# Sections in a norm, attention batches without a mutual wait, a slack in a planner and more idle matmuls: one kernel, four changes at once

## The chip, the cores and the metric

The kernel runs on one core of a Trainium2 chip. The metric is the device time of one execution in microseconds (us), lower is better. A "fast run" is an execution that shows no slow state; all runs below are fast but one of h1_normg. Ratios to the kernel before, with their 95% intervals in brackets, are taken from runs of the same rounds and are not quite the ratio of the medians that are quoted. In lines of the profile, PE is TensorE and PEld its loading of weights, ACT is ScalarE, DVE VectorE, POOL GpSimd and SP SyncE; SPq is the DMA queue of SP. The granted clock is the share of full clock that TensorE was given.

## The reference

Eight batches of linear attention with an RMS norm, and behind it a channel mixing of two branches:

```python
kv  = einsum('bhsd,bhse->bhde', k, v)              # 8 batches, 8 heads, 576 rows, 64 wide
o   = einsum('bhsd,bhde->bhse', q, kv)
x   = o / sqrt(mean(o*o, -1) + 1e-6) * g_norm      # per head; then heads side by side: 512 wide
xk  = mu_k*x + (1-mu_k)*x_prev                     # x_prev: the row before in the same batch
xr  = mu_r*x + (1-mu_r)*x_prev
out = sigmoid(xr @ w_r) * (max(xk @ w_k, 0)**2 @ w_v)   # 512 -> 1024 -> 512
```

In the kernel, "K", "V" and "R" are the matmuls with w_k, w_v and w_r, done for nine groups of 512 rows; "kv", "u", "st" (sums of squares), "rr" (the norm factor spread over a head's partitions) and "x" are the steps of attention, done for each of eight batches. A group needs one or two finished batches.

## The kernel before

The kernel is written as pieces of work. A planner in Python simulates them while the kernel is built, with a cost for each piece, a model of DMA, and a number of buffers for each name; its only product is which engine takes a piece and the order of the instructions on each engine. The order is then fixed: each engine takes its instructions one after the other, and one that has to wait holds up all behind it.

```python
class Planner:
    LAT = {"PE": 0.25, "ACT": 0.15, "DVE": 0.12, "POOL": 0.15, "SP": 0.0}
    SWITCH = {"PE": 0.11, "ACT": 1.28}
    SHUN = {"DVE": 0.5}
    STAY = {"PE": 4.0, "ACT": 4.0}
    # ... run():
                for eng, us in p.on.items():
                    t = max(free.get(eng, 0.0), room)          # engine free, buffers free
                    for d in p.deps:
                        t = max(t, d.end + (self.LAT[d.eng] if d.eng != eng or d.land else 0.0))
    # ... the earliest start wins; among those within 0.02 us of it, the smallest "due"
            if p.land:                                          # a DMA: when does it land?
                came = p.end + 1.2
                if p.eng == "POOL":                             # loads, one after the other
                    dma = max(dma, came) + p.land
                    p.end = dma + 0.8
                else:                                           # stores and transposing DMAs, on SP
                    p.end = max(came + p.land, min(dma, came + 2 * p.land)) + 0.8
                    dma = max(dma, came) + p.land
```

Until the first R matmul, gaps of TensorE in the plan are filled with matmuls of zeros ("idle matmuls"), which keep its clock up. The attention of a batch waits, besides its loads, for the last rr of the batch before (`last_rr[b - 1]`). Batches 0 to 2 have q transposed on TensorE, batches 3 to 7 by a DMA. The norm of a whole batch, four head pairs by 576 rows, works on one tile of 128 x 576, of which eight rows hold something:

```python
        mm = add({"PE": 0.25 * n}, kv_mm, mode=1, bufs=[pkv, kin, vin, kv], due=due(26),
                 deps=[loaded[...] ...] + [last_rr[b - 1]])
        # ...
        if b >= 3:
            m = add({"SP": 3.2}, q_dma, bufs=[qin, qT], due=due(30), deps=[loaded[("q", b, 0)]], land=2.5)
        # ... st_act:
            nc.scalar.activation(out=get(ln)[:, 0:wide, 0:w], in_=pst.t[:, 0:wide, 0:w], func=AF.Ln, bias=eps, scale=1.0 / HD)
            nc.scalar.activation(out=get(rs)[:, 0:wide, 0:w], in_=ln.t[:, 0:wide, 0:w], func=AF.Exp, scale=-0.5)
        st = add({"ACT": 0.42 + 0.0018 * sec}, st_act, deps=[m], bufs=[pst, ln, rs], due=due(17), mode="ln")
```

Of the kernel before, what the change touches and what calls it, by code (L numbers as in the profile page):

```python
# [25 lines left out]
class Piece:  # L26
    def __init__(self, on, fn, deps, bufs, due, land, mode):
        self.on, self.fn, self.due, self.land, self.mode = on, fn, due, land, mode
        self.deps = [d for d in deps if d is not None]
        self.bufs = list(bufs)  # L30
        for b in self.bufs:
            b.users.append(self)
        self.eng = self.start = self.end = None


class Planner:
# [3 lines left out]
    SHUN = {"DVE": 0.5}  # L40
    STAY = {"PE": 4.0, "ACT": 4.0}
# [5 lines left out]
    def add(self, on, fn, deps=(), bufs=(), due=0.0, land=0.0, mode=None):  # L47
        p = Piece(on, fn, deps, bufs, due, land, mode)
        self.left.append(p)
        return p  # L50
# [24 lines left out]
    def run(self, warm=None):  # L75

        free, order, dma, modes = {}, [], 0.0, {"PE": None, "ACT": None}
        while self.left:
            best = {}
            for p in self.left:  # L80
                if any(d.end is None for d in p.deps):
                    continue
                room = self.room(p.bufs)
                if room is None:
                    continue
                ways = []
                for eng, us in p.on.items():
                    t = max(free.get(eng, 0.0), room)
                    for d in p.deps:
                        t = max(t, d.end + (self.LAT[d.eng] if d.eng != eng or d.land else 0.0))  # L90
                    ways.append((t + us + self.SHUN.get(eng, 0.0), t, eng))
                _, t, eng = min(ways)
                stay = self.STAY.get(eng, 0.0) if p.mode == modes.get(eng) else 0.0
                best.setdefault(eng, []).append((t, p.due - stay, p))
# [5 lines left out]
            if warm and p.eng == "PE":  # L100
                since, until, idle = warm
                n = int((t - max(free.get("PE", 0.0), since)) / 0.23)
                if n > 0:
                    order.append(lambda n=n: idle(n))
                if p is until:
                    warm = None
# [29 lines left out]
def kernel(  # L136
# [22 lines left out]
    HS = S // 2  # L159
    NI = NJ // 2  # L160
# [18 lines left out]
        "ln": (1, (128, 2, HS), FP32),  # L179
        "rs": (2, (128, 2, HS), BF16),  # L180
# [41 lines left out]
    g_st = const.tile([128, 128], FP32, name="g_st")  # L222
    eps = const.tile([128, 1], FP32, name="eps")
    zeros = const.tile([128, 512], BF16, name="zeros")
    sel2 = const.tile([128, 32], BF16, name="sel2")
    selg = const.tile([128, NHP, 128], BF16, name="selg")
# [7 lines left out]
    def consts_small(_):  # L234
        nc.vector.memset(zeros, 0.0)
        nc.vector.memset(g_st, 0.0)
        nc.sync.dma_start(out=mu_raw[0:NHP], in_=moe_mu_k.rearrange("(j p) -> j p", p=128))
        nc.sync.dma_start(out=mu_raw[NHP:2 * NHP], in_=moe_mu_r.rearrange("(j p) -> j p", p=128))
        g_row = g_norm.rearrange("(o d) -> o d", o=1)
        for hp in range(NHP):  # L240
            for e in range(2):
                nc.sync.dma_start(out=g_st[32 * hp + e:32 * hp + e + 1, HD * e:HD * e + HD], in_=g_row)
        nc.vector.memset(eps, 1e-6)
        nc.vector.memset(selg, 0.0)

        nc.vector.memset(sel2, 0.0)
        for e in range(2):
            nc.vector.memset(sel2[64 * e:64 * e + 64, e:e + 1], 1.0)
        ln_table()
# [6 lines left out]
    def consts_mu(_):  # L256
# [5 lines left out]
        for hp in range(NHP):  # L262
            rows = slice(32 * hp, 32 * hp + 32)
            nc.vector.tensor_copy(out=selg[rows, hp, :], in_=g_st[rows])
# [4 lines left out]
    add({"DVE": 0.9}, consts_small, due=-1000)  # L269
# [6 lines left out]
    def load(b, n, h0, h1, due):  # L276
# [6 lines left out]
        p = add({"POOL": 0.8}, fn, bufs=[kvq[(n, b)]], due=due, land=(h1 - h0) * 0.36)  # L283
# [5 lines left out]
    for hp0, n in PARTS0:  # L289
        for name in ("k", "v", "q"):  # L290
            load(0, name, 2 * hp0, 2 * hp0 + 2 * n, -900 + hp0)
        if p_ident is None:
            p_ident = add({"POOL": 0.8}, consts_idents, due=-900 + 0.5)
    p_mu = add({"DVE": 0.5}, consts_mu, deps=[p_ident], bufs=[p_mu_ps], due=-800)
    p_wr = add({"POOL": 0.8}, lambda _: load_w(w_r_sb, moe_w_r), due=-700, land=2.6)
    p_wk = add({"POOL": 0.8}, lambda _: load_w(w_k_sb, moe_w_k), due=-699, land=5.2)
    for n in ("k", "v", "q"):
        load(1, n, 0, H, -698)
    p_wv = add({"POOL": 0.8}, lambda _: load_w(w_v_sb, moe_w_v), due=-697, land=5.2)
# [6 lines left out]
    last_rr = {-1: None, 0: None}  # L306
# [14 lines left out]
    def attention_part(b, part, bufs, ps_buf):  # L321
# [26 lines left out]
        def kv_copy(eng, e):  # L348
            for half in range(2):
# [3 lines left out]
        mm = add({"PE": 0.25 * n}, kv_mm, mode=1, bufs=[pkv, kin, vin, kv], due=due(26),  # L353
                 deps=[loaded[(m, b, h)] for m in ("k", "v") for h in (2 * hp0, 2 * (hp0 + n) - 1)] + [last_rr[b - 1]])
        kvs = [add({"DVE": 0.25 + 0.14 * n, "ACT": 0.38 + 0.11 * n}, lambda eng, e=e: kv_copy(eng, e), deps=[mm],
# [4 lines left out]
        if b >= 3:  # L360
# [4 lines left out]
            m = add({"SP": 3.2}, q_dma, bufs=[qin, qT], due=due(30), deps=[loaded[("q", b, 0)]], land=2.5)  # L365
            qts = {hp: m for hp in hps}
        else:
            for hp in hps:
# [7 lines left out]
                def q_cp(eng, hp, ps):  # L376
# [3 lines left out]
                m = add({"PE": 0.35}, lambda _, hp=hp, ps=ps: q_tr(_, hp, ps), bufs=[ps, qin, qT], due=due(27),  # L380
                        deps=[p_ident, loaded[("q", b, 2 * hp)], loaded[("q", b, 2 * hp + 1)], last_rr[b - 1]])
                qts[hp] = add({"ACT": 0.65, "DVE": 0.75}, lambda eng, hp=hp, ps=ps: q_cp(eng, hp, ps), deps=[m],
# [4 lines left out]
        for hp in hps:  # L387
# [17 lines left out]
            m = add({"PE": 0.14}, lambda _, hp=hp, ps=ps: u_mm(_, hp, ps), mode=1, deps=kvs + [qts[hp]],  # L405
                    bufs=[ps, kv, qT, uT, sq], due=due(22))
            us[hp] = add({"ACT": 0.69, "DVE": 0.75}, lambda eng, hp=hp, ps=ps: u_cp(eng, hp, ps), deps=[m],
                         bufs=[ps, uT], due=due(21))
            sqs.append(add({"DVE": 0.46}, lambda eng, hp=hp: u_sq(eng, hp), deps=[us[hp]], bufs=[uT, sq],
                           due=due(20)))  # L410



        nsec = NHP // n
        sec = S // nsec
        pst = ps_buf()
        wide = 2 if sec > 512 else 1
        w = sec // wide

        def st_mm(_):  # L420
            for x in range(wide):
                for i, hp in enumerate(hps):
                    for c in range(nsec):
                        row = 32 * (i * nsec + c)
                        nc.tensor.matmul(get(pst)[row:row + 32, x, 0:w], sel2,  # L425
                                         sq.t[:, hp, sec * c + w * x:sec * c + w * x + w], start=True, stop=True)

        def st_act(_):
            ln_table()
            nc.scalar.activation(out=get(ln)[:, 0:wide, 0:w], in_=pst.t[:, 0:wide, 0:w], func=AF.Ln, bias=eps,  # L430
                                 scale=1.0 / HD)
            nc.scalar.activation(out=get(rs)[:, 0:wide, 0:w], in_=ln.t[:, 0:wide, 0:w], func=AF.Exp, scale=-0.5)

        m = add({"PE": 0.3}, st_mm, mode=2, deps=sqs, bufs=[pst, sq, ln, rs], due=due(18))
        st = add({"ACT": 0.42 + 0.0018 * sec}, st_act, deps=[m], bufs=[pst, ln, rs], due=due(17), mode="ln")


        xms = []
        step = min(2, n)
        for hp1 in range(hp0, hp0 + n, step):  # L440
            for half in range(2):
# [3 lines left out]
                def rr_mm(_, hp1, half, ps):  # L445
                    for i in range(step):
                        c0 = HS * half
                        while c0 < HS * half + HS:
                            c, off = divmod(c0, sec)
                            x, off = divmod(off, w)  # L450
                            cnt = min(HS * half + HS - c0, w - off)
                            nc.tensor.matmul(get(ps)[:, i, c0 - HS * half:c0 - HS * half + cnt],  # L452
                                             selg[:, (hp1 - hp0 + i) * nsec + c, :], rs.t[:, x, off:off + cnt],
                                             start=True, stop=True)
                            c0 += cnt

                def x_mul(_, hp1, cs, xs, ps):
                    if xT.t is None:
# [7 lines left out]
                m = add({"PE": 0.13 * step}, lambda _, hp1=hp1, half=half, ps=ps: rr_mm(_, hp1, half, ps),  # L466
                        deps=[st, p_mu], bufs=[ps, rs, xT], due=due(14))
                xms.append(add({"DVE": 0.15 + 0.3 * step},
# [11 lines left out]
        df = add({"DVE": 0.4 * n}, diff, deps=xms, bufs=[xT, d], due=due(11))  # L480
# [3 lines left out]
        for pos, (key, dst, m) in enumerate(order):  # L484
# [15 lines left out]
            sc = add({"DVE": 0.365 * n, "ACT": 0.7 * n}, lambda eng, m=m, t=t: scale(eng, m, t), deps=[df, p_mu], bufs=[d, t], due=late)  # L500
            x_ready[b][key].append(add({"DVE": 0.06 + 0.34 * n}, lambda _, dst=dst, t=t: blend(_, dst, t), deps=[sc],
# [18 lines left out]
    p_first = add({"PE": 0.01}, lambda _: None, deps=x_ready[0]["r"] + [p_wr], bufs=[warm], due=-1)  # L520
    hold = add({"PE": 0.01}, lambda _: None, bufs=[warm], due=-2000)

    def mix(g):
# [23 lines left out]
        for f2 in range(NFC // 2):  # L547
            ps, rt, u = Buf("mm"), Buf("relu"), k0 + 2 * f2
            ms = []
            for x in range(2):  # L550
                ms.append(add({"PE": 0.865}, lambda _, fc=2 * f2 + x, ps=ps: k_mm(_, fc, ps),
                              deps=ms or need["k"] + [p_wk], bufs=[ps, sqk], due=u + x))
            a = add({"ACT": 1.04}, lambda _, ps=ps, rt=rt: k_relu(_, ps, rt), deps=ms[1:], bufs=[ps, rt], due=u + 2)
            sqs.append(add({"DVE": 0.7}, lambda _, f2=f2, rt=rt: k_sq(_, f2, rt), deps=[a], bufs=[rt, sqk], due=u + 4))
# [13 lines left out]
        for c2 in range(2):  # L568
            ps, sg, u = Buf("mm"), Buf("sig"), r0 + 2 * c2
            ms = []  # L570
            for x in range(2):
                ms.append(add({"PE": 0.865}, lambda _, ci=2 * c2 + x, ps=ps: r_mm(_, ci, ps),
                              deps=ms or need["r"] + [p_first], bufs=[ps, sg], due=u + x))
            sigs.append((sg, add({"ACT": 1.04}, lambda _, ps=ps, sg=sg: r_sig(_, ps, sg), deps=ms[1:], bufs=[ps, sg],
# [11 lines left out]
        for c2 in range(2):  # L586
# [3 lines left out]
            for x in range(2):  # L590
                for part in range(2):
                    ms.append(add({"PE": 0.865},
                                  lambda _, ci=2 * c2 + x, part=part, ps=ps: v_mm(_, ci, part, ps),
                                  deps=ms[-1:] or sqs + [p_wv, sg_done.deps[0]], bufs=[ps, sqk, ot], due=u + 2 * x + part))
            for xs in ((0, 2),) if g < NG - 1 else ((0, 1), (1, 2)):
                dv = add({"DVE": 0.12 + 0.56 * (xs[1] - xs[0])},
# [45 lines left out]
```

## Time and profile before

| | before |
|---|---|
| time | 239.06 us (median of 3 runs, 238.25 to 239.2) |
| span of the profiled run | 236.1 us |
| TensorE busy | 214.8 us, 91% |
| first R matmul | 28.2 us |
| end of the last V matmul | 231.7 us |

From the page of the kernel before, TensorE's busy time, its busy tenths in 40 slices of 5.9 us, the granted clock in tenths, and what DMA moved in each slice:

```profile
PE 214.8 (91%) x1538; PEld 100.4 (43%) x1538; DVE 137.3 (58%) x233; ACT 136.1 (58%) x184; POOL 25.2 (11%) x39
...
PE   2988999579987999989998998999899999999971
...
PEclk9999999857997999999999999999999999999997
...
GB/s 80 187 209 206 204 207 204 203 182 189 199 194 222 193 163 175 224 149 160 270 82 3 90 89 0 3 120 60 0 12 162 9 41 137 0 37 143 0 89 89
```

TensorE is busy almost throughout, and the clock line says where this is not full rate: slices 8, 9, 10 and 13, counted from one (41 to 59 us and 71 to 77 us). DMA moves about 200 GB/s until 100 us (163 to 224 in slices 2 to 17), and another line of the page has its engines busy 90% or more in these slices, all but the 15th.

The timeline of TensorE before, between 40 and 59 us (start, duration, line, operation, result <- operands, count, and in brackets the idle time before and what ended it):

```profile
40.34 1.90 PE L537 MATMUL mm<-xk,w_k 128*128 128x512 bf16 x8
43.93 0.65 PE L452 MATMUL at<-rs,selg 128*128 128x288 bf16 x4 [1.69 <-ACT rs L432]
45.18 0.40 PE L452 MATMUL at<-rs,selg 128*128 128x288 bf16 x2 [0.60 <-DVE xT L461]
...
49.26 1.49 PE L343 MATMUL at<-v,k 96*64 96x64 bf16 x48
...
52.30 1.08 PE L393 MATMUL at<-qT,kv 64*64 64x288 bf16 x7 [0.59 <-ACT kv L205]
53.31 1.89 PE L537 MATMUL mm<-xk,w_k 128*128 128x512 bf16 x4
...
58.62 1.03 PE L580 MATMUL mm<-w_v,sqk 128*128 128x512 bf16 x4
```

K of group 0 ends at about 42 us, and then only attention of batches 1 and 2 is left, in small pieces between waits: first for the norm on ScalarE (1.69 us), then for xT on VectorE. K of group 1 starts at 53.31 and V of group 0 at 58.62. The granted clock falls with the gaps.

The same view in a later batch: rr is eight matmuls, and the last four wait, two by two, for a buffer that x on VectorE has to free.

```profile
102.58 0.40 PE L452 MATMUL at<-rs,selg 128*128 128x288 bf16 x2 [0.60 <-DVE xT L461]
103.25 0.41 PE L452 MATMUL at<-rs,selg 128*128 128x288 bf16 x2 [0.26 <-DVE xT L461]
```

And what became of the q of batch 3: the transposing DMA on SP's queue starts at 53.44, and the load that waits for its end starts at 65.92 on POOL; the k load of batch 5 comes at 70.15.

```profile
53.44 6.82 SPq L362 DMA_TRANSPOSE qT<-q  x1
```

```profile
65.92 0.77 POOL L278 DMA_DIRECT2D q<-in_q_dram  x1 [13.33 <-DMA qT<-q]
...
70.15 0.77 POOL L278 DMA_DIRECT2D k<-in_k_dram  x1
```

TensorE asks for this q at 69.78 us, 4 us after it has landed.

```profile
69.78 0.44 PE L393 MATMUL at<-qT,kv 64*64 64x288 bf16 x8
```

### The profile page before, as it was taken

What the parts mean: (1) busy time and instruction counts of PE and PEld (TensorE: products, weight loads), DVE (VectorE), ACT (ScalarE), POOL (GpSimd) and SP (SyncE); (2) the same over time, 40 slices, a digit from 0 to 9 for tenths busy, and PEclk for the clock granted to TensorE, in tenths of its full rate; (3) what the DMA queues carried; (4) which work ended last, traced back from release to release, by engine and by line L of the source; (5) the groups of instructions that cost most, each with busy time, mean ns of one, the idle gap of its engine ahead of it and who ended that gap; (6) DMA issues with size and microseconds to landing.
All of it is one profiled execution on the core that took longest, in us unless ns stands there. A gap on an engine that the chain in (4) does not pass through costs nothing.

```text
span 236.1 us, 3800 instructions
## 1 busy us (share of the span) xinstructions
PE 214.8 (91%) x1538; PEld 100.4 (43%) x1538; DVE 137.3 (58%) x233; ACT 136.1 (58%) x184; POOL 25.2 (11%) x39
## 2 busy tenths in 40 slices
PE   2988999579987999989998998999899999999971
PEld 1443453253442453444444484434344444444430
DVE  2127936597698498379729953985596224224221
ACT  2075788585366857786688668855953603604500
POOL 8833030040031021001000000000000000000000
PEclk9999999857997999999999999999999999999997
DMA  5999999999999979999930320042005014015033
GB/s 80 187 209 206 204 207 204 203 182 189 199 194 222 193 163 175 224 149 160 270 82 3 90 89 0 3 120 60 0 12 162 9 41 137 0 37 143 0 89 89
DMA packets 38497, 29.41 MB, mean 125 GB/s; under 512 B 13384, under 2 KB 33360, under 8 KB 38480
## 3 DMA queue, kind: packets, MB, share of 16 engines
q0 software_dynamic: 21008, 16.78, 47.2%
q1 hardware_dynamic: 17472, 12.40, 23.1%
q8 instruction: 12, 0.20, 0.4%
q14 instruction: 5, 0.04, 0.1%
HBM read 33.56 MB, written 9.44 MB: 182 GB/s over the span
## 4 chain that ended last, share of the span: by engine, by line
PE 79%; DVE 10%; ACT 6%; issue 2%; POOL 1%; DVEq 0%; POOLq 0%
PE mm L537 27%; PE mm L580 25%; PE mm L560 12%; DVE xT L461 5%; PE mm L609 5%; PE at L393 3%; PE at L452 2%; PE at L343 2%; DVE out L584 2%; ACT t L493 1%; DVE d L478 1%; PE at L425 1%; ACT ln L430 1%; PE at L373 1%; ACT kv L205 1%
## 5 line engine op out<-in xcount | busy, mean ns | idle before, releaser
L537 PE MATMUL mm<-xk,w_k 128*128 128x512 bf16 (+1 forms) x320 | 69.2, 367 | 0.1
L580 PE MATMUL mm<-w_v,sqk 128*128 128x512 bf16 x288 | 65.5, 379 | 2.0 <-DVE out L584 1.7
L541 ACT ACTIVATE relu<-mm 128x1024 bf16<-128x1024 f32 x36 | 36.9, 1024 | 39.8 <-PE mm L537 39.1
L537 PEld LDWEIGHTS <-w_k 128*128 128x128 bf16 x320 | 30.0, 99 | 31.4 <-issue 4.0
L580 PEld LDWEIGHTS <-sqk 128*128 128x128 bf16 x288 | 27.6, 97 | 34.7 <-issue 3.7
L544 DVE TENSOR_TENSOR sqk<-relu 128x1024 bf16<-128x1024 bf16 x36 | 24.9, 691 | 29.4 <-ACT relu L541 29.4
L584 DVE TENSOR_TENSOR out<-mm,sig 128x1024 f32<-128x1024 f32 (+1 forms) x20 | 22.3, 1116 | 25.0 <-PE mm L580 24.9
L560 PE MATMUL mm<-w_r,xr 128*128 128x512 bf16 x144 | 32.9, 380 | 0.0
L461 DVE TENSOR_TENSOR xT<-uT,at 128x576 bf16<-128x576 bf16 (+1 forms) x31 | 21.1, 731 | 17.0 <-PE at L452 16.9
L493 ACT ACTIVATE t<-d,mu_sb 128x576 bf16<-128x576 bf16 x34 | 23.7, 764 | 4.0 <-DVE d L478 2.4
L560 PEld LDWEIGHTS <-xr 128*128 128x128 bf16 x144 | 13.5, 98 | 16.7 <-issue 1.3
L565 ACT ACTIVATE sig<-mm 128x1024 bf16<-128x1024 f32 x18 | 17.9, 1024 | 4.3 <-PE mm L560 4.2
L205 ACT CAST uT<-at 128x576 bf16<-128x576 f32 x23 | 13.9, 641 | 10.0 <-PE at L393 10.0
L609 PE MATMUL mm<-zeros 128*128 128x512 bf16 x64 | 18.0, 410 | 0.0
L452 PE MATMUL at<-rs,selg 128*128 128x288 bf16 (+1 forms) x62 | 11.1, 285 | 6.1 <-DVE xT L461 4.3
L205 ACT CAST kv<-at 64x256 bf16<-64x256 f32 x24 | 8.8, 366 | 12.9 <-PE at L343 12.5
L402 DVE TENSOR_TENSOR sq<-uT 128x576 bf16<-128x576 bf16 x32 | 13.9, 455 | 3.2 <-ACT uT L205 2.8
L278 POOL DMA_DIRECT2D q<-in_q_dram x10 | 7.5, 751 | 48.5 <-DMA qT<-q 31.4
L452 PEld LDWEIGHTS <-selg 128*128 128x128 bf16 x68 | 6.5, 97 | 12.9 <-issue 10.3
L393 PE MATMUL at<-qT,kv 64*64 64x288 bf16 x116 | 9.1, 316 | 2.8 <-ACT uT L205 0.9
L496 DVE TENSOR_TENSOR xk<-t,xT 128x2304 bf16<-128x2304 bf16 (+2 forms) x10 | 11.2, 1116 | 0.5 <-ACT t L493 0.4
L478 DVE TENSOR_TENSOR d<-xT 128x2304 bf16<-128x2304 bf16 (+2 forms) x10 | 11.2, 1119 | 0.3
(52 smaller groups left out, 135.0 us busy)
## 6 DMA issues: line engine op xcount, KB each, us to landing
out_dram<-out SPq DMA_DIRECT2D x24, 192.0 KB
k<-in_k_dram POOLq DMA_DIRECT2D x7, 576.0 KB, 14.3
v<-in_v_dram POOLq DMA_DIRECT2D x7, 576.0 KB, 16.4
q<-in_q_dram POOLq DMA_DIRECT2D x7, 576.0 KB, 7.7
out_dram<-out SPq DMA_DIRECT2D x24, 128.0 KB
out_dram<-out SPq DMA_DIRECT2D x24, 64.0 KB
w_k<-in_moe_w_k_dram POOLq DMA_DIRECT2D x1, 1024.0 KB, 12.3
w_v<-in_moe_w_v_dram POOLq DMA_DIRECT2D x1, 1024.0 KB, 23.3
```

The lines of the kernel that those rows point to most:

```text
L205: nc.scalar.copy(out=dst, in_=src)
L452: nc.tensor.matmul(get(ps)[:, i, c0 - HS * half:c0 - HS * half + cnt], selg[:, (hp1 - hp0 + i) * nsec + c, :], rs.t[:, x, off:off + cnt], ...
L461: nc.vector.tensor_mul(out=xT.t[:, hs, xs], in0=get(uT)[:, hs].rearrange("q h i jj p -> q h (i jj p)")[:, :, cs], in1=ps.t[:, 0:step, 0:HS])
L493: nc.scalar.mul(out=dst, in_=d.t[:, hp, :], mul=by)
L537: nc.tensor.matmul(get(ps)[:, fc % 2, a0:a1], w_k_sb[:, cc, 128 * fc:128 * fc + 128], xk[:, cc, x0:x0 + a1 - a0], start=(cc == 0), stop=(c ...
L541: nc.scalar.activation(out=get(rt), in_=ps.t, func=AF.Relu)
L544: nc.vector.tensor_mul(out=get(sqk)[:, 2 * f2:2 * f2 + 2, :], in0=rt.t, in1=rt.t)
L560: nc.tensor.matmul(get(ps)[:, ci % 2, :], xr[:, cc, n0:n0 + 128], w_r_sb[:, cc, :], start=(cc == 0), stop=(cc == NHP - 1))
L565: nc.scalar.activation(out=get(sg), in_=ps.t, func=AF.Sigmoid)
L580: nc.tensor.matmul(get(ps)[:, ci % 2, :], sqk.t[:, fc, 128 * ci:128 * ci + 128], w_v_sb[:, fc, :], start=(fc == 0), stop=(fc == NFC - 1))
L584: nc.vector.tensor_mul(out=get(ot)[:, xs, :], in0=ps.t[:, xs, :], in1=sg.t[:, xs, :])
L609: nc.tensor.matmul(get(warm)[:, 0, :], zeros[:, 0:128], zeros, start=True, stop=True)
```

## The change

Four things in one: (1) the norm is cut into four sections of 144 columns, so that ln and exp work on 128 x 144 (with a second buffer for ln); (2) only batch 1 waits for the rr of the batch before, the others run free; (3) the planner reckons 0.3 us of slack on everything that TensorE waits for; (4) the idle matmuls go on after the first R matmul, until 80 us of planned time, in the buffer that the next piece will write. The intent is a shorter norm, more freedom for the planner, and an order that waits less on the chip. The diff, cut to its core (names for the pieces and constants left out):

```diff
+    SLACK = {"PE": 0.3}
...
-                    t = max(free.get(eng, 0.0), room)
+                    slack = self.SLACK.get(eng, 0.0)
+                    t = max(free.get(eng, 0.0), room + slack)
                     for d in p.deps:
-                        t = max(t, d.end + (self.LAT[d.eng] if d.eng != eng or d.land else 0.0))
+                        t = max(t, d.end + (self.LAT[d.eng] + slack if d.eng != eng or d.land else 0.0))
...
+                gap = t - max(free.get("PE", 0.0), since)
+                if first is not None:
+                    n, buf = int(gap / 0.23), None
+                else:
+                    n, buf = int((gap - 0.3) / 0.23), p.bufs[0] if p.fresh and not p.bufs[0].placed else None
+                    n = n if buf is not None and t < until else 0
...
-    last_rr = {-1: None, 0: None}
+    last_rr = {}
...
-        mm = add(... deps=[loaded[...] ...] + [last_rr[b - 1]])
+        mm = add(... deps=[loaded[...] ...] + ([last_rr[0]] if b == 1 else []))
...      # the q transposes likewise
-        m = add({"PE": 0.3}, st_mm, mode=2, deps=sqs, bufs=[pst, sq, ln, rs], due=due(18))
-        st = add({"ACT": 0.42 + 0.0018 * sec}, st_act, ...)
+            for s in range(NHP):
+                for i, hp in enumerate(hps):
+                    tl, sub = place(i, s)
+                    nc.tensor.matmul(get(pst)[32 * tl:32 * tl + 32, 0, 0:SEC], sel[:, sub],
+                                     sq.t[:, hp, SEC * s:SEC * s + SEC], start=(sub == 0), stop=(sub == n - 1))
+            nc.scalar.activation(out=get(ln), in_=pst.t[:, 0, 0:SEC], func=AF.Ln, bias=eps, scale=1.0 / HD)
+            nc.scalar.activation(out=get(rs), in_=ln.t, func=AF.Exp, scale=-0.5)
+        st = add(f"rs {b}", {"ACT": 0.7}, st_ln, ...)
...
-                nc.sync.dma_start(out=g_st[32 * hp + e:32 * hp + e + 1, HD * e:HD * e + HD], in_=g_row)   # 8 of them
+        nc.sync.dma_start(out=g_all, in_=g_norm.rearrange("(o d) -> o d", o=1).broadcast_to([128, HD]))
...
-    plan.run((1.5, p_first, idle))
+    plan.run((1.5, p_first, 80.0, idle))
```

## The prediction

> # Prediction
>
> **What bounds it now.** TensorE: 214.8 of 236.1 us busy (page, part 1), 79% of the chain that ended last. By the timeline, 32 back-to-back 512-column matmuls take 6.91 us, 0.216 each (the Trainium skill, "TensorE: Matmul & The Clock Gate", Back-to-back issue gap, gives N/2.4 + 2.5 ns; the trace agrees). Nine groups of K, R and V, 80 such matmuls each, make 155.5 us. A batch of attention costs TensorE 0.88 (kv) + 1.1 (u) + 0.36 (statistics) + 0.9 (rr) = 3.25 us, and 1.3 us of transposes in batches 1 and 2: 25.5 us for seven. So 181 us of work lie between the first R (28.2 us) and the last V (231.7): about 22 us are lost there. Where, by timeline and windows:
> - 42 to 53.3 us: batch 1's blend is not done, batch 2 waits for batch 1's last rr. 3.2 us of work in 11.3: 8 lost. Granted clock 0.50 from 46 to 54.
> - 53 to 60: 1 us. 69.8 to 76.5: u waits for copies, then K at clock 0.5: 4 us.
> - Batches 3 to 6: 22.36 us a period against 17.3 + 3.25: 1.8 each, 7.4 us. Most is rr, 2.3 us instead of 0.9, as its at buffers wait for DVE xT (0.60 + 0.26 us).
> - Two waits of 0.84 us for DVE out at the end.
>
> **What the change does.**
> 1. Sectioned norm: ln and exp shrink from 128x576 (740 + 682 ns) to 128x144 (380 + 322 ns, as batch 0 shows). 0.72 us less ACT per batch, seven times, in each norm chain. TensorE's columns stay (8x288 becomes 16x144, twice); perhaps +0.1 us a batch. The selg build (four broadcast multiplies, estimated 0.6 to 0.8 us each from 691 ns for 128x1024 bf16 and 1222 for 128x1024 f32) falls in DVE's idle 5 to 11 us: free.
> 2. Batches from 2 on don't wait for the previous rr. Batch 2's loads land only about 39 to 44 us, so its kv comes some 5 us sooner, not more; it fills part of the hole.
> 3. Slack for TensorE: the planner puts V or K between rr pieces and before u. Takes most of the steady loss.
> 4. Idle matmuls until 80 us of planned time keep the clock up (same page, Part 1: a few us of idle halve the clock; here 0.50 after the gap at 42 to 44). Some will overstay; at the start the slack lengthens planned gaps, so the first R may come up to 1 us later.
>
> **Sum**, all where TensorE is critical: hole at 42 to 60: -4; 69 to 77: -2.5; steady: -4.5; start: +0.5; tail: 0. About -10.5. **Predicted 228.5 us, range 222 to 235.** Faster by over 2% 0.87, within 2% 0.10, slower by over 2% 0.03.
>
> **What would show it.** ln and rs at 380 and 322 ns throughout; PE's wait for xT at rr from 4.3 us to under 1.5; period of batches 3 to 6 about 21.2 us; more than 64 zeros matmuls, some after 30 us; clock 0.9 or more from 30 to 80 us; first K of group 1 before 52 us; first R at 28 to 29.
>
> **What would make it wrong.** Batch 2's copies (earlier due times) crowd DVE and ACT ahead of batch 1's blend, so the hole only moves; idle matmuls run while real work is ready; group 0's last squares, queued behind attention on DVE (relu done 44.8, square at 55), still block V; DMA, full until about 100 us, bounds batches 2 to 4; more ACT table loads (now 12 of 1.28 us).

## The result

The kernel after takes 245.51 us (median of 4, 245.15 to 247.04) against 239.13 us in the same rounds: ratio 1.0282, 95% interval 1.0228 to 1.0337. It is slower by 2.8%, where a gain of 4.4% was foreseen.

The page of the kernel after, the same lines (slices of 6.1 us):

```profile
PE 213.6 (88%) x1688; PEld 104.9 (43%) x1688; DVE 142.3 (58%) x246; ACT 125.5 (52%) x175; POOL 25.1 (10%) x39
...
PE   3999899899009989989999899999989999999981
...
PEclk9999999999657999999999999999999999999997
...
GB/s 43 198 209 205 204 207 204 204 204 200 161 177 184 255 172 198 206 213 76 6 156 110 3 112 62 3 0 175 0 0 117 58 0 172 3 11 164 0 86 86
```

TensorE's busy time is 1.2 us less in a span 7.2 us longer. Slices 11 and 12, counted from one (60.8 to 73.0 us), have a 0: TensorE stands still. The timeline of TensorE around it:

```profile
56.60 0.95 PE L354 MATMUL at<-v,k 96*64 96x64 bf16 x48
...
59.96 0.43 PE L433 MATMUL at<-sq,sel 128*32 128x144 bf16 x16
73.56 0.46 PE L404 MATMUL at<-qT,kv 64*64 64x288 bf16 x4 [13.17 <-DMA qT<-q]
...
74.35 1.17 PE L456 MATMUL at<-rs,selg 128*128 128x144 bf16 x8
75.31 1.06 PE L540 MATMUL mm<-xk,w_k 128*128 128x512 bf16 x2
```

Four u matmuls of batch 3, queued right behind the statistics of batch 2, wait 13.17 us for the DMA that transposes q. Behind them in the queue stand all of K of group 1 (its first piece starts at 75.31; before, it started at 53.31) and the rr of batch 2, though xk of batch 1 had been ready since 57.26 us. The chain that ended last, the profile's walk back from the last instruction to what released each one, says the same in its own columns (start, duration, what):

```profile
54.81 18.61 DMA qT<-q
73.43 0.14 issue
73.56 0.46 PE at L404 x4
```

The queues of SP and POOL, as shown of before:

```profile
54.81 7.88 SPq L373 DMA_TRANSPOSE qT<-q  x1
```

```profile
47.17 0.77 POOL L288 DMA_DIRECT2D k<-in_k_dram  x1 [2.31 <-PE at L354]
47.93 0.77 POOL L288 DMA_DIRECT2D v<-in_v_dram  x1
57.86 0.77 POOL L288 DMA_DIRECT2D k<-in_k_dram  x1 [9.15 <-PE at L354]
58.62 0.77 POOL L288 DMA_DIRECT2D v<-in_v_dram  x1
73.98 0.77 POOL L288 DMA_DIRECT2D q<-in_q_dram  x1 [14.60 <-DMA qT<-q]
```

The transposing DMA starts at 54.81, 1.4 us later than before, and lands at 73.43, 18.6 us after its start. Before, the load released by it came at 65.92, 12.5 us after its start. The difference is in what the queue of loads holds. In both kernels loads of batch 4 were still on their way when the transposing DMA was issued (1.6 MB of them before and 1.4 MB after, from a count of the bytes moved until then), but in the kernel after k and v of batch 5 came on top at 57.86 (1.18 MB), since the free-running kv of batch 3 had released their buffers early.

The kept trace has every DMA packet with its queue, size and time, which the views above do not split. The transposing DMA is 2304 packets of 256 B, and the first of them starts 4.0 us after the issue in both kernels. As long as loads are queued beside it, its packets and theirs (768 B) go one for one: 611 and 606 from 58.5 to 62 us before, 1383 and 1311 from 63 to 71 us after. Before, the loads ran out at 63.8 us, the rest of the transposing DMA then went at about 1000 packets a us instead of some 175, and its last packet was done at 64.7 us. After, the loads of batch 5 kept the turns going, and its last packet was done at 71.1 us, 2.4 us before the landing that TensorE saw. The Trainium skill ("DMA: Bandwidth & Descriptors", Queues, rings and completion order) says that each DMA engine takes turns between the queues that have work, packet by packet; the trace agrees, by these counts.

What the planner believed can be read from its own schedule, which is computed when the kernel is built (engine, start, end, piece, in its own microseconds; it is no measurement):

```
SP      50.51   59.00 qT dma 3
PE      58.38   58.79 st 2
PE      59.30   59.55 u 3
PE      60.19   60.56 rr 2
PE      61.20   62.07 K 1
```

So it queued u 0.30 us behind a landing that it had at 59.00 and that came at 73.43. In the plan of the kernel before that landing stands at 59.00 too, but u of batch 3 stood at 66.48, as kv had to wait for the rr of batch 2. The plan's own time runs ahead of the chip's here (it issues that DMA at 50.51, the chip at 54.81), so the plain error is one of duration: 8.5 us planned, 18.6 measured. Before, it was there as well, 8.5 planned against 12.5, and cost nothing.

Other lines that answer to those of before: ln and exp, by shape, in the kernel after (count, then busy us and mean ns):

```profile
L612 PE MATMUL mm<-zeros 128*128 128x512 bf16 x81 | 22.2, 406 | 0.0
...
L438 ACT ACTIVATE ln<-at,eps 128x144 f32<-128x144 f32 x10 | 3.8, 381 | 3.7 <-PE at L433 3.7
...
L439 ACT ACTIVATE rs<-ln 128x144 bf16<-128x144 f32 x10 | 3.2, 323 | 0.3
```

They take 381 and 323 ns in all ten places, and the zeros matmuls number 81 and some more in other buffers (94 planned, 64 before). The first R matmul comes at 32.00 us in the timeline, instead of 28.05 (32.17 and 28.22 in the chain). In the batches from 3 on, R of one group follows R of the group before after 20.9 us in the mean (89.17 to 172.78 us, four periods), against 22.1 before (76.48 to 164.89 us). TensorE's waits for xT in rr fell as foreseen, here from the view of waits (us in total, times, longest), first before, then after with its one long wait:

```profile
PE at L452 <- DVE xT L461: 4.3, 10, 0.6
```

```profile
PE at L404 <- DMA qT<-q: 13.2, 1, 13.2
...
PE at L456 <- DVE xT L464: 1.8, 3, 0.6
```

The steady batches of this order thus gained about what was foreseen, the start lost 4 us, and one wait lost 13.

### The profile page after: what moved, and what is told of

Same layout as the page of the kernel before. It is cut to its first block, busy times and chain, and to the rows that moved or that the text cites. A ratio compares the mean times of both kernels' runs of the same rounds, so it can differ in the third digit from the quotient of the medians.

```text
span 243.3 us, 4092 instructions
## 1 busy us (share of the span) xinstructions
PE 213.6 (88%) x1688; PEld 104.9 (43%) x1688; DVE 142.3 (58%) x246; ACT 125.5 (52%) x175; POOL 25.1 (10%) x39
## 4 chain that ended last, share of the span: by engine, by line
PE 81%; DMA 8%; DVE 5%; ACT 2%; issue 1%; POOL 1%; DVEq 0%; ACTq 0%; POOLq 0%
PE mm L540 27%; PE mm L583 25%; PE mm L563 13%; DMA qT<-q 8%; PE mm L612 6%; PE at L456 3%; PE at L404 2%; DVE xT L464 2%; PE at L354 1%; PE at L384 1%; PE at L433 1%; PE at L612 1%; ACT kv L216 1%; DVE out L587 1%; ACT sig L568 1%
## 5 line engine op out<-in xcount | busy, mean ns | idle before, releaser
L540 PE MATMUL mm<-xk,w_k 128*128 128x512 bf16 (+1 forms) x320 | 67.1, 360 | 0.7 <-ACT relu L544 0.7
L496 ACT ACTIVATE t<-d,mu_sb 128x576 bf16<-128x576 bf16 x33 | 23.2, 766 | 17.4 <-DVE d L481 16.0
L464 DVE TENSOR_TENSOR xT<-uT,at 128x576 bf16<-128x576 bf16 (+1 forms) x31 | 21.7, 731 | 14.4 <-PE at L456 14.3
L216 ACT CAST uT<-at 128x576 bf16<-128x576 f32 x20 | 12.2, 639 | 23.5 <-PE at L404 23.5
L612 PE MATMUL mm<-zeros 128*128 128x512 bf16 x81 | 22.2, 406 | 0.0
L404 PE MATMUL at<-qT,kv 64*64 64x288 bf16 x116 | 7.4, 303 | 13.2 <-DMA qT<-q 13.2
L612 PEld LDWEIGHTS <-zeros 128*128 128x128 bf16 x94 | 8.7, 102 | 11.2 <-issue 3.9
L456 PE MATMUL at<-rs,selg 128*128 128x144 bf16 x120 | 11.4, 233 | 1.8 <-DVE xT L464 1.8
L456 PEld LDWEIGHTS <-selg 128*128 128x128 bf16 x128 | 9.9, 101 | 6.6 <-issue 2.4
L404 PEld LDWEIGHTS <-kv 64*64 64x64 bf16 x128 | 2.8, 104 | 21.7 <-issue 21.6
## 6 DMA issues: line engine op xcount, KB each, us to landing
w_v<-in_moe_w_v_dram POOLq DMA_DIRECT2D x1, 1024.0 KB, 22.4
```

What stands on the lines that cost most here:

```text
L404: nc.tensor.matmul(t[64 * e:64 * e + 64, jj, 0:NI * NP], kv.t[js, hp, e, :], qT.t[js, 2 * hp + e, :], start=True, stop=True)
L456: nc.tensor.matmul(get(ps)[:, i, SEC * c:SEC * c + SEC], selg[:, tl, sub].rearrange("p e d -> p (e d)"), rs.t, start=True, stop=True)
L464: nc.vector.tensor_mul(out=xT.t[:, hs, xs], in0=get(uT)[:, hs].rearrange("q h i jj p -> q h (i jj p)")[:, :, cs], in1=ps.t[:, 0:step, 0:HS])
L496: nc.scalar.mul(out=dst, in_=d.t[:, hp, :], mul=by)
L540: nc.tensor.matmul(get(ps)[:, fc % 2, a0:a1], w_k_sb[:, cc, 128 * fc:128 * fc + 128], xk[:, cc, x0:x0 + a1 - a0], start=(cc == 0), stop=(c ...
L612: nc.tensor.matmul(get(buf or warm)[:, 0, :], zeros[:, 0:128], zeros, start=True, stop=True)
```

## The experiments

Seventeen kernels were run. The kernel before ran beside each (medians from 238.5 to 239.4 us). Theory A: the loss is TensorE work queued behind DMA that lands later than the planner believes. Its rivals: B, DMA supply binds whatever the order; C, the longer start and the idle matmuls are the loss; D, free running costs by its order on ScalarE and VectorE.

### First four: take the stall away in three ways, and the start

**e1_deps.** Free running undone.

```diff
-    last_rr = {}
+    last_rr = {-1: None}
-... + ([last_rr[0]] if b == 1 else [])
+... + [last_rr[b - 1]]            # kv and the q transposes
```

> The kernel after, with the wait of every batch's attention on the rr of the batch before restored (free running undone). Theory A (the loss is one stall of TensorE: u of batch 3 is queued behind nothing but a transposing DMA that the planner believed done at 59 us and that landed at 73.4): u of batch 3 is queued late again, the 13.2 us wait is gone, PE waits for qT under 1 us; 232 to 236 us, a part of the gain of the steady batches lost. Theory B (DMA supply binds batches 2 to 4, whatever the order): the wait moves to another place, 243 us or more. Theory C (the longer start and the idle matmuls are the loss): 243 us or more, first R at 32 us as in after.

Measured: 234.61 us, ratio to before 0.9837 (0.9794 to 0.988). No wait of TensorE for DMA over 0.6 us is left. Free running costs 10.9 us in the company of the rest, and the kernel after without it is faster than before, by 1.6%.

**e2_land.** The plan's landing of that one DMA moved.

```diff
                     dma = max(dma, came) + p.land
+                    p.end += 10.0 * (p.name == "qT dma 3")
```

> The kernel after, free running kept; only the planner is told that the transposing DMA of batch 3 lands 10 us later (69 instead of 59 us in its own time). Not one instruction is added or taken away by that but idle matmuls; the order on the engines changes. Theory A: the 13.2 us wait falls to under 4 us, 231 to 235 us. Theory B: as much waiting elsewhere in 55 to 75 us, 243 us or more. Theory C: 243 us or more.

Measured: 240.59 us, ratio 1.0088 (1.0033 to 1.0143): outside what either theory had said. TensorE's timeline of this kernel:

```profile
60.44 0.43 PE L434 MATMUL at<-sq,sel 128*32 128x144 bf16 x16
...
65.58 1.43 PE L355 MATMUL at<-v,k 96*64 96x64 bf16 x48 [4.39 <-DMA v<-in_v_dram]
```

The stall of u is gone and another one is in its place: kv of batch 4 waits 4.39 us for its v. The plan had it right behind its landing, too.

**e3_pe3.** q of batch 3 transposed on TensorE.

```diff
-        if b >= 3:
+        if b >= 4:
```

> The kernel after, with batch 3's q transposed on TensorE, as in batches 0 to 2, and not by DMA (batches 4 to 7 stay on DMA): the wait is taken away with its cause. TensorE gets 24 transposes (about 1.1 us) and ACT or DVE four copies (0.64 or 0.46 us each). Theory A: 231 to 235 us, no wait of u for qT over 2 us. Theory B: q of batch 3 still arrives at 54 us and loads stay full, so about as much waiting: 240 us or more. Theory C: 243 us or more.

Measured: 240.1 us, ratio 1.0049 (1.0011 to 1.0087), at the edge of what B had said (240 or more), and again there is a stall for the next late load, v of batch 5:

```profile
82.81 0.43 PE L354 MATMUL at<-v,k 96*64 96x64 bf16 x9 [6.36 <-DMA v<-in_v_dram]
```

So A was too narrow: not one landing is reckoned too early, but those of q of batch 3, v of batch 4 and v of batch 5, and each takes its turn when the one ahead of it is mended.

**e4_start.** The slack left out of the plan until the first R.

```diff
-                    slack = self.SLACK.get(eng, 0.0)
+                    slack = self.SLACK.get(eng, 0.0) if not warm or warm[1] is None else 0.0
```

> The kernel after, with the 0.3 us of slack for TensorE left out of the plan until the first R matmul is placed. It tests the start alone: if the slack (and the idle matmuls planned from it) made the first R 4 us later, it comes at 28 to 28.7 us; if the broadcast load of g_norm, which moved 128 packets among the first loads, did it, it stays at 30 us or more. On the total, theory A says that the stall for batch 3's transposing DMA, which lands when DMA lets it, swallows most of this: 240 to 245 us. Theory C says the gain is kept: 241.5 us or less with the stall unchanged at about 13 us.

Measured: 241.66 us, ratio 1.0116 (1.0084 to 1.0147). The first R comes at 28.6 us, against 32.0 in the kernel after: the late start is the slack's, which lengthens the planned gaps that are then filled with idle matmuls. The total lies within the range of A and just outside that of C, and as the order changed, so did the stalls (4.6 us for q of batch 3, 4.5 us for v), so this run settles the start and nothing else.

### The parts one by one

**f4_norm.** Only the new norm on top of the kernel before.

```diff
 (the kernel after, with the waits of e1_deps restored and)
-    SLACK = {"PE": 0.3}
+    SLACK = {"PE": 0.0}
-    plan.run((1.5, p_first, 80.0, idle))
+    plan.run((1.5, p_first, 0.0, idle))
```

> Only the norm in sections (with its constants): the waits on the batch before restored, slack 0, no idle matmuls after the first R. It is the kernel before plus the new norm. Against before: 0.72 us less ACT per batch on the norm chain, TensorE 16 pieces of 144 columns for 8 of 288, the g_norm broadcast delaying first loads. If the prediction's step 1 is right: 1 to 4 us faster than before, 235 to 238 us. A rival: the shorter pieces and the g_norm load cost what ACT gains: 238 to 240 us.

Measured: 230.95 us (229.74 to 231.87), ratio 0.9678 (0.9627 to 0.9728). The norm alone gains 7.5 us, more than the 5.0 us that 0.72 us in each of seven batches gives in all. It is the best kernel whose gain is clear. Its timeline in the place of the old hole:

```profile
41.70 0.43 PE L433 MATMUL at<-sq,sel 128*32 128x144 bf16 x16
42.06 2.15 PE L583 MATMUL mm<-w_v,sqk 128*128 128x512 bf16 x8
44.93 0.66 PE L456 MATMUL at<-rs,selg 128*128 128x144 bf16 x8 [0.71 <-ACT rs L439]
45.43 1.89 PE L583 MATMUL mm<-w_v,sqk 128*128 128x512 bf16 x8
```

V of group 0 now stands directly behind the statistics of batch 1 and fills the hole; before, its first matmul came at 58.62. In the window from 42.2 to 60 us TensorE is busy 15.42 us at a mean clock of 0.90, against 13.76 us at 0.71 before.

**g1_order.** Is that the shorter ln and exp, or the order that the planner makes of a smaller figure?

```diff
 (the kernel before, old norm)
-        st = add({"ACT": 0.42 + 0.0018 * sec}, st_act, ...)
+        st = add({"ACT": 0.7}, st_act, ...)
```

> The kernel before, its norm as it was (ln and exp of 128x576, 740 + 682 ns); only the planner's figure for the pair is set to the 0.7 us that it has for the new norm (it was 1.46 us). The order that the planner makes is then nearly that of f4_norm, which took 230.95 us. If f4_norm's 7.5 us came from the order (V of group 0 fills the hole at 42 to 53 us, as the last relu no longer waits behind table load, ln and exp): 231 to 234 us. If they came from the time that ACT saves on the chip: 237 us or more.

Measured: 234.53 us, ratio 0.9824 (0.9794 to 0.9854); between the two expectations. A figure in the planner, wrong for the chip, gains 4.0 us, as V of group 0 fills the hole here as well; the other 3.6 us come only with the new norm itself (the first R is 1.4 us later here too, 29.41 against 28.05). The same place in this kernel shows part of the difference, a wait for the long exp:

```profile
43.43 2.16 PE L580 MATMUL mm<-w_v,sqk 128*128 128x512 bf16 x8
47.01 0.65 PE L452 MATMUL at<-rs,selg 128*128 128x288 bf16 x4 [1.43 <-ACT rs L432]
```

It is 1.43 us here and 0.71 us in f4_norm, and the 0.72 us between them is what ln and exp lost in length.

**g2_free.** f4_norm plus free running.

> f4_norm (230.95 us) plus the free-running batches alone: no slack, no later idle matmuls. The planner reckons it 4.1 us faster than f4_norm (last multiply ends at 221.1 against 225.3 us of its own time). If free running is what costs, by TensorE work queued right behind DMA landings: PE waits of 5 us or more for a load or a transposing DMA between 55 and 85 us and 236 to 244 us. If it only hurt together with the slack: 227 to 231 us.

Measured: 240.03 us, ratio 1.0068 (1.0028 to 1.0108): 9.1 us more than f4_norm. TensorE waits 5.6 us for the transposing DMA of batch 3 and 1.2 us for a v:

```profile
PE at L404 <- DMA qT<-q: 5.6, 1, 5.6
```

This is a wait of 5 us or more, as was expected, without any slack. The two make 6.8 of the 9.1 us.

**g3_slack.** f4_norm plus the slack.

> f4_norm plus the slack of 0.3 us for TensorE alone (no free running, no later idle matmuls; the longer planned gaps at the start still fill with idle matmuls before the first R). e1_deps, which has the later idle matmuls too, took 234.6. The prediction had the slack at -4.5 us in the steady batches and +0.5 at the start. By the planner's own time it costs 5.0 us (230.2 against 225.3). If the slack is the cost: 233.5 to 236 us, first R at 31.5 to 32.2. If the later idle matmuls were: 231 us or less.

Measured: 234.12 us, ratio 0.9805 (0.9775 to 0.9836): 3.2 us more than f4_norm. The first R comes at 32.5 us. The gain on rr that the prediction gave to the slack is there without it: f4_norm, with slack 0, waits 1.8 us in all for xT at rr, as the kernel after does. From the fourth R to the sixth a period takes 22.4 us before, 21.9 in f4_norm, 21.3 here, 20.9 in g2_free and 21.1 in the kernel after. In these steady batches the slack thus adds some 0.6 us a batch to what the norm gains, and it loses more than that elsewhere.

**g4_idle.** f4_norm plus the later idle matmuls.

> f4_norm plus the idle matmuls until 80 us of planned time alone (15 more of them by the plan, about 3.2 us of TensorE time if none finds a real gap). Granted clock between 40 and 80 us rises to 1.00 in most slices. If they fall into real gaps: 229 to 231 us; if they overstay: 232 to 234 us.

Measured: 232.0 us, ratio 0.9722 (0.9692 to 0.9751): 1.0 us more than f4_norm, at the border of the second expectation. The intervals of the two ratios overlap (0.9627 to 0.9728 for f4_norm), so this is not clear of the scatter. The clock is kept at full between 42 and 60 us, and nothing is won by it.

### Is it the lateness or the order?

**f2_margin.** Free running with a margin in the plan.

```diff
+                        far = 10.0 if eng == "PE" and d.land and d.name[-1] in "34567" else 0.0
-                        t = max(t, d.end + (...))
+                        t = max(t, d.end + far + (...))
```

> The kernel after, free running kept; in the plan alone, TensorE pieces that need a load or a transposing DMA of batches 3 to 7 are reckoned 10 us later than that landing. e2_land and e3_pe3 only moved the stall from u to kv of batch 4, which then waited 4.4 and 6.4 us for its v. Theory A in its wider form (free running lets the planner queue TensorE work right behind DMA landings that it reckons 4 to 14 us too early; TensorE runs in order, so all behind waits): waits of PE for any DMA after 40 us fall under 2 us in sum, total 233 to 237 us. Theory D (free running costs for another reason: early copies of later batches crowd ACT and DVE ahead of batch 1 and 2): no DMA waits, yet 239 us or more, PE waiting for ACT or DVE or filled with idle matmuls.

Measured: 235.83 us, ratio 0.9885 (0.9847 to 0.9923). No wait for DMA is left among TensorE's waits, and 9.7 of the 10.9 us are back, with free running kept. Theory A in its wider form holds here.

**h2_freemargin.** The same margin without slack and idle matmuls.

> g2_free (norm and free running, 240.0 us) with the planner's 10 us of margin on what TensorE needs from DMA in batches 3 to 7; no slack, no later idle matmuls. If free running costs only where TensorE is queued behind a load that the plan has landing too early: no PE wait for DMA over 1 us after 40 us, and 229 to 232 us, as f4_norm (230.95). If free running has another cost of its own: 233 us or more with those waits gone.

Measured: 243.19 us, ratio 1.017 (1.0098 to 1.0241). A miss: 10 us was not margin enough in this order. From its view of TensorE's waits:

```profile
PE at L355 <- DMA v<-in_v_dram: 7.6, 2, 6.3
...
PE at L405 <- DMA qT<-q: 2.8, 1, 2.8
```

The longest is at 97 us, for v of batch 6. The waits that the run should have removed were there, so it could not tell A from D.

**i2_norm_noload, i1_free_noload, i3_after_noload.** The orders of f4_norm, of g2_free and of the kernel after, without the loads of batches 2 to 7; the plan is the same line by line.

```diff
         def fn(_):
+            if b >= 2:
+                kvq[(n, b)].t = kvq[(n, b - 2)].t      # read the older batch again
+                return
             nc.gpsimd.dma_start(out=get(kvq[(n, b)])..., ...)
```

> The order of f4_norm (norm alone, 230.95 us) without the loads of batches 2 to 7 (wrong result on purpose); the base for i1_free_noload. f4_norm waits for loads less than 1 us after the start, so the loads' absence should change little: 227 to 231 us.

> The order of g2_free (norm and free running, 240.0 us) instruction for instruction on the compute engines, with the loads of k, v and q for batches 2 to 7 left out: those batches read the tiles of batches 0 and 1 again (wrong result on purpose). DMA lateness is taken away, the order stays. If free running costs only where TensorE waits for late DMA: this is faster than i2_norm_noload by 1 to 4 us (the plan says 4.1). If the order has a cost of its own (copies and squares of later batches ahead of nearer work on ACT and DVE): slower than i2_norm_noload by 2 us or more.

> The kernel after, whole, without the loads of batches 2 to 7 (wrong result on purpose). If its loss to e1_deps (245.5 against 234.6 us) is DMA lateness met by an early order: the 13.2 us wait is gone and it takes 230 to 235 us. If the order costs by itself: 238 us or more.

Measured (wrong results): 230.61, 230.27 (runs from 227.54 to 230.63) and 232.46 us; ratios 0.9654 (0.9594 to 0.9713), 0.9609 (0.9545 to 0.9673) and 0.9725 (0.9693 to 0.9757). With nothing late, free running costs nothing that these runs can tell: i1 and i2 are the same within their intervals, which are some 1.2% wide, and D falls. It gains nothing clear either; the 4.1 us that the planner sees in it do not appear. The kernel after loses 13.0 us of its 245.5 with the loads gone, and the wait was 13.2 us. The longest wait of TensorE for DMA in i3 is

```profile
PE at L357 <- DMA v<-in_v_dram: 0.5, 1, 0.5
```

The loads matter little to f4_norm (0.3 us), so B, that their supply binds every order, falls as well.

### Smaller ones

**f1_deps_start.** e1_deps and e4_start together.

> The kernel after with two parts undone: the waits on the batch before (as in e1_deps) and the slack until the first R (as in e4_start). e1_deps gave 234.6 with its first R at 31.9 us. If the late start is worth its 3.3 us once no stall for DMA swallows it: 231 to 232 us. If the DMA supply of batches 2 and 3 (loads land when they land) takes it back: 234 to 235 us.

Measured: 234.1 us, but from 231.37 to 234.42 in four runs, ratio 0.9787 (0.9724 to 0.9851). Its median is within 0.5 us of that of e1_deps. Its first R stands at 29.4 us, 2.4 us before that of e1_deps, and the end is not earlier. It lies in the second range that was expected, but TensorE has no wait for DMA here, so the reason given there is not shown; by the starts of R it is still ahead at the fourth (114.90 against 119.04) and level at the fifth (140.04 against 139.95). The planner's own end for it is only 0.4 us earlier than for e1_deps (229.9 against 230.2).

**f3_grow.** The broadcast load of g_norm replaced.

```diff
-        nc.sync.dma_start(out=g_all, in_=g_norm...broadcast_to([128, HD]))
+        nc.sync.dma_start(out=g_row, in_=g_norm.rearrange("(o d) -> o d", o=1))
+        nc.vector.memset(ones_row, 1.0)
 ...
+        nc.tensor.matmul(pg, ones_row, g_row, start=True, stop=True)
+        nc.vector.tensor_copy(out=g_all, in_=pg)
```

> The kernel after, with the broadcast load of g_norm (128 packets of 256 B, during which the first loads of k moved about 120 KB less a microsecond) replaced by a load of one row, spread over partitions by a matmul with ones. If those packets hold up the loads: the kv matmul of batch 0 can start about 1.5 us earlier (k landed about 8.1 us after the start in after, 6.2 in before), all loads land 1 to 2 us earlier, the wait of 13.2 us is 1 to 2 us shorter, total 243.5 to 245 us. If not: 245.5 us and the same landing times. The first R stays at 31.5 to 32.2 us, being set by planned idle matmuls.

Measured: 244.44 us, ratio 1.0242 (1.0197 to 1.0286); 1.1 us less than the kernel after, but the intervals of the two ratios overlap (1.0228 to 1.0337), so the gain is not clear of the scatter. What is clear is the earlier data. The page's line of what DMA moved:

```profile
GB/s 82 187 200 205 204 206 204 204 204 164 141 156 138 191 200 192 191 204 117 162 157 95 3 134 43 0 3 173 0 0 126 50 0 175 1 14 162 0 87 87
```

Its first slice has 82 GB/s, as before the change (80), where the kernel after has 43. The transposing DMA of batch 3 starts at 53.43 instead of 54.81 and the wait for it is 10.1 us. The small broadcast load thus was one more cause of late data; the first R is unmoved (32.4 us).

**h1_normg.** The same in f4_norm.

> f4_norm with the broadcast load of g_norm replaced by one row and a matmul with ones. In f3_grow that took 1 us off the kernel after. A version meant to beat both kernels: 229.5 to 231 us if the early loads matter here, 231 if the start is held by the idle matmuls of the plan anyway.

Measured: 233.0 us, runs from 230.36 to 234.49, one of them slow; ratio 0.9763 (0.9712 to 0.9815). That ratio does not come out of its three fast runs alone: their mean, 232.12 over 239.01, gives 0.971. Inconclusive against f4_norm's 0.9678: the fastest run is as fast, the median is not, and no cause of the scatter was found.

### The sum

| kernel | us | against before in the same rounds |
|---|---|---|
| f4_norm: norm | 230.95 | -7.5 |
| g4_idle: norm, idle matmuls | 232.0 | -6.5 |
| g3_slack: norm, slack | 234.12 | -4.4 |
| g2_free: norm, free running | 240.03 | +1.6 |
| e1_deps: norm, slack, idle matmuls | 234.61 | -4.2 |
| after: all four | 245.51 | +6.4 |

Added to f4_norm one at a time, the idle matmuls, the slack and free running cost 1.0, 3.2 and 9.1 us (differences of medians, so good to about 1 us); -7.5 + 1.0 + 3.2 + 9.1 = +5.8, close to the +6.4 of all together. The cost of free running belongs to the order at hand, not to free running as such: with a margin in the plan it was 1.2 us in f2_margin (235.83 against 234.61) and 12.2 in h2_freemargin (243.19 against 230.95), by the loads that the order ran into.

## Why the prediction was wrong

- *"Batches from 2 on don't wait for the previous rr ... its kv comes some 5 us sooner, not more; it fills part of the hole."* This is the step that failed. The kv of batch 2 did come sooner (45.92 us against 49.26), but the same freedom let the planner queue u of batch 3 right behind a DMA for which it reckoned 8.5 us and which took 18.6, and all of TensorE's work waited 13.2 us behind it. Instead of part of a gain of 4 us, free running costs 9.1 us alone and 10.9 in company. The prediction named DMA "full until about 100 us" as a danger and costed it at nothing. It looked at when data arrives, and not at what stands behind the instruction that waits for it.
- *"Slack ... Takes most of the steady loss", -4.5, and "start: +0.5".* The start was mis-sized: it lost 4.0 us (28.05 to 32.00), not 0.5, since slack on each of a chain of pieces adds up and idle matmuls fill it; e4_start shows the cause. The period of the steady batches came out as predicted (20.9 us against about 21.2), but only in part by the slack: the shorter waits at rr are there in f4_norm without it, and of the 1.3 us a batch the norm alone gives 0.5, and the slack on top of it some 0.6 (g3_slack). Alone, the slack costs 3.2 us.
- *"Sectioned norm: 0.72 us less ACT per batch."* Right in its durations (381 and 323 ns), too small in effect: 7.5 us. About 4 us are an effect on the order that the prediction did not see, V of group 0 moved into the hole, which g1_order gets with the old norm. The prediction had seen that hole and what blocked V in it, the last squares queued behind attention, but as a danger and not as the prize.
- *"Idle matmuls until 80 us keep the clock up."* Where TensorE has queued work they do so, and it is worth nothing on top of the norm (g4_idle, +1.0 us, not clear of the scatter). In the one long wait there were none: the planner saw no gap there. The clock was at 0.50 from about 62.9 to 76.5 us. The Trainium skill ("TensorE: Matmul & The Clock Gate", Part 1: The HAM clock gate) gives about 3.4 us of idleness before the clock is halved; here TensorE stopped at 60.4 us, and the granted clock was 1.00 up to 62, 0.72 in the mean from 62 to 64 and 0.50 from then on. If it fell from 1.00 to 0.50 at once, it did so at about 62.9 us (an estimate from the 0.72), some 2.5 us after the stop: of the page's size, but sooner, and the measurement decides. The trace's record of the clock has the change at 62.89. In the kernel before it has one at 45.61 us, and there TensorE was not idle for more than 1.69 us at a time.
- *Signs named in advance:* ln and rs times, waits at rr (1.8 us, "under 1.5" was close), the period and the zeros matmuls were right. The first K of group 1 "before 52 us" came at 75.3, the first R "at 28 to 29" at 32.0, and the clock "0.9 or more from 30 to 80" was 0.50 for over 13 us: these three point at the stall and the start.

## What to carry to other kernels

When work is moved ahead on an engine that runs in order, ask what it will wait for and what stands behind it: a wait that cost nothing at the end of a queue costs its whole length in front of it. A planner that knows DMA only roughly needs either a margin where an engine waits for DMA or a dependency that happens to give one; before such a dependency is taken out as useless, look in the trace by how much the data really comes ahead of its use (here 4 us, with a planned 7.5). And a change of four parts deserves four runs: one part here was worth 7.5 us, and the other three took it and more.

## What the Trainium skill lacked or had wrong

- "DMA: Bandwidth & Descriptors" (Bandwidth, Latency and other measured facts, DMA Transpose) has no figure for how long a transposing DMA takes to land while loads are queued on another queue. Here it was 18.6 us with some 2.6 MB of loads queued before or soon after it, about 12.5 us with 1.6 MB, and 5.2 us in the least case, against the planner's 8.5.
- The same page warns of transfers under 512 B as below line rate, but not that one small broadcast, 128 packets of 256 B that all read one row, holds up the loads beside it: the first slice moved 43 GB/s with it and 82 GB/s without (f3_grow).
- "TensorE: Matmul & The Clock Gate", Back-to-back issue gap, gives about 131 ns per matmul of 512 columns as a sustained rate beside an isolated gap of about 216 ns. In this case's traces 32 back-to-back matmuls, with loads of weights between them, took 6.91 us, 216 ns each: the figure that the section keeps for the isolated gap, and which the prediction used, holds for the stream.
- The same page, Part 1: The HAM clock gate, has about 3.4 us of idleness before the clock is halved. Here it was halved some 2.5 us after TensorE stopped, and in the kernel before without an idle time above 1.69 us.
- "ScalarE: Activation LUTs", What ACT_TABLE_LOAD costs, has 1283 ns for the load, which the trace shows to the nanosecond, and some 1380 ns of draining with it. In f4_norm a relu ends at 42.82 us, the load runs from 42.85 to 44.13 and ln starts at 44.14: no such draining shows.
- No page says what an idle matmul costs when the gap that it was planned for is not there; here 15 more of them by plan cost about 1.0 us (g4_idle against f4_norm), which is not clear of the scatter.
